# First chunk of `w_in` loaded first, min(r, 1)^2 of eight chunks as a square on ScalarE, other work shares

## The chip, the cores and the metric

The kernel runs on one core of one Trainium2 chip. The metric is the device time of one execution in microseconds (us). Engines are named as in the profile: PE is TensorE's matmul, PEld its weight load, DVE is VectorE, ACT is ScalarE, POOL is GpSimd, SP is SyncE, which here only issues DMAs.

## The reference

Sigmoid attention for 8 batches of 12 heads (448 tokens, head width 64), followed by a two-layer MLP over all 3584 tokens. The activation between the two layers is 0 below -1, h above 1, and (h+1)^2/4 between.

```python
scores = scale * np.matmul(q, k.transpose(0, 1, 3, 2)) - np.log(S)
attn = 1.0 / (1.0 + np.exp(-scores))
x = np.ascontiguousarray((attn @ v).transpose(0, 2, 1, 3)).reshape(B * S, H * D)
h = x @ w_in                       # 768 -> 2048
g = np.where(h >= 1, h, np.where(h <= -1, 0.0, (h + 1) ** 2 / 4.0))
return g @ w_out                   # 2048 -> 768
```

## The kernel before

**Tiling.** One batch is one tile of 448 tokens. Two heads make a pair (48 pairs, six for a batch). For each pair, `scores` fills `psc` from K and Q in three pieces of 128 keys and one of 64, ACT takes the sigmoid in `weigh` (L454 or L457), and `av` adds the product with V into `pav`; ACT copies it to `x32` (L504) and DVE takes its largest value (L508). The hidden width is 16 chunks of 128. For a batch, `up` (L722, or `up_blocks` L688 from batch 2 on, a scheme with seven instead of eight products) makes h of each chunk in PSUM (`ph`, three banks shared with `po`), `bend` turns h into g and splits g into two f16 halves `ghl`, and `down` (L758) adds the chunks into `po`, which DVE scales into `o` (L768).

**Two f16 halves.** Nearly every matmul runs on high and low f16 halves, three products each. So each operand needs a largest value, a scale, a rounded copy (mostly ACT) and a remainder (mostly DVE, `SCALAR_TENSOR_TENSOR`).

**The weights.** They come as 64-bit words. `Weight.load` (L202) fetches a chunk of 768 KB, and `Weight.convert` makes f32 of it: ACT takes the absolute value (L224), a clamp follows (L226, on POOL for chunks 0, 2, 4 and 6, later on DVE; or together with the maximum in L236), and three DVE operations of 768 columns put the bits together (L241, L244, L247). Eight chunks of `w_in` have their bound summed by ACT (L218). `find_scale` and `split` then make the f16 halves (L286, L287, or L282 to L284 on POOL).

**The order in time.** Batch 0's attention (f32 matmuls, pairs 0 to 5) runs beside the conversion of `w_in`; when its six pairs are done, `finish_x(0)` scales x. Then batch 0's 16 chunks of `up` and its first-half `down` run, interleaved with batch 1's attention and the conversion of `w_out`: 72 units in all, and `B0`, `B1` say over which of them the attention steps are spread. Batch 1's MLP is interleaved with batch 2's attention up to `LAST1` units before its end, and with `mix`, which prepares the blocks of `w_in` that `up_blocks` reads. From batch 2 on each batch does 56 block units and 48 `down` units beside the next batch's attention. `L0`, `A0`, `LSTEP` say at which attention step pairs 8 and 9 are loaded and prepared ahead of time.

**Shares.** `prep_a` finds the largest or summed absolute values of a pair from 8 on: for pairs below `MAX_ACT` by ACT with a sum (L344, two or three instructions), for the others by DVE with `tensor_reduce` (L346, two instructions). `prep_b` splits q, k and v of a pair: by ACT and DVE below `QA` (L373, L374), by POOL above (L378 to L380).

**What sets the order.** SP's first loads are written out by hand; within an engine, a list scheduler places the rest by priority and its own estimate of time, so the order of instructions changes everywhere when a part changes. Each engine runs its list in order: an instruction that waits holds back all behind it.

`bend` before, for a chunk whose h stands in PSUM: ACT makes r in `g` by a Relu with a bias (L735); DVE makes min(r, rt)·r (L736), where rt is the value that stands for 1; DVE takes the larger of that and h times a factor (L737), which is the last reader of the PSUM bank; ACT rounds (L738); DVE takes the remainder (L739).

Of the kernel before, what the change touches and what calls it, by code (L numbers as in the profile page):

```python
# [14 lines left out]
F32 = mybir.dt.float32  # L15
# [3 lines left out]
AF = mybir.ActivationFunctionType  # L19
ALU = mybir.AluOpType  # L20
# [18 lines left out]
LAST = 84  # L39
LAST1 = 18  # L40
WI_A = 14
# [3 lines left out]
B0 = 9  # L45
B1 = 66
GPOOL = 1
POOL_FROM = 6
WI_SUM = 2
WO_SUM = 0  # L50
MAX_ACT = 47
L0 = 9
A0 = 19
LSTEP = 3

SB = 2
CLAMP = 7
QA = 17
QT = 3
WOP = 6  # L60
MIXP = 0
CORN = 10
TP = 1

DW = 8
# [10 lines left out]
def sigmoid_attention_mlp(ctx: ExitStack, tc: tile.TileContext, first_qvk, qkv, w_in, w_out, out_t):  # L76
# [102 lines left out]
    class Weight:  # L179


        def __init__(self, dram, sb, name, spare):
            self.dram, self.sb, self.name, self.spare = dram.bitcast(I32), sb, name, spare
            self.words, self.at, self.loaded = {}, 0, 0
            self.scale, self.inv = [], []
            self.most = const.tile([P, 2, NFC], F32, name=name + "_most")
            nc.vector.memset(self.most, 0.0)
            mod = WI_SUM if name == "wi" else WO_SUM
            self.summed = [f for f in range(NFC) if mod and f % mod == 0 and f not in (NA - 1, NFC - 1)]

# [19 lines left out]
        def convert(self):  # L210

            f = self.at - 2
            if 0 <= f < NFC:
                w = self.words.pop(f)
                if f in self.summed:

                    dump = wo.f32(-1) if self is wi else w[:, :DM].bitcast(F32)
                    nc.scalar.activation(dump, self.f32(f), AF.Abs, accum_out=self.most[:, 1, f : f + 1])  # L218
                if self is wo:
                    self.load(3 if f == 3 else 1)  # L220
# [33 lines left out]
        def find_scale(self):  # L254
# [4 lines left out]
            nc.vector.tensor_reduce(out=m, in_=self.most[:, :, GROUPS[k]], axis=AX.X, op=ALU.max)  # L259
            c, e = m[:, 0:1], sml_p.tile([P, 1], F32, tag="wx", name=name + "_x", bufs=1)  # L260
            ci, ei = c.bitcast(I32), e.bitcast(I32)
# [291 lines left out]
    def small(tag, in0, s1, op0, s2=None, op1=None, ints=False):  # L553
        t = sml_p.tile([P, 1], F32, tag=tag, name=tag, bufs=2 if tag.startswith("od") else 1)
# [43 lines left out]
    def common_scales(b, inv_x, ih=None):  # L598

        big = [largest(inv_x, k) for k in range(2)]  # L600
        q = [small("q%d" % k, big[k][1], wo.root[k], ALU.mult) for k in range(2)]
        q = small("qm", q[0], q[1], ALU.min)
        for k in range(2):
            up_sc[b, k] = up_scales(ih or big[k][0], small("rk%d" % k, q, wo.iroot[k], ALU.mult), k)
        od = inverse("od", small("qq", q, q, ALU.mult))
        down_sc[b, None] = lambda: od
# [19 lines left out]
    def mix(i):  # L626
# [25 lines left out]
        for t0, n, chunk, k in ((0, 2, f, 0), (2, 1, g, 1)):  # L652
            src = w_in_sb[:, chunk].rearrange("p h (t n) -> p h t n", t=2)[:, :, 2 - n :, :]
            for h in range(2):
                nc.vector.tensor_scalar(
                    out=pv[:, h, t0 : t0 + n, :], in0=src[:, h], scalar1=to[k], scalar2=None, op0=ALU.mult
                )
        nc.sync.dma_start(out=blocks[i][:, : 3 * DM], in_=pl)
# [70 lines left out]
    def bend(b, f, h):  # L729
# [4 lines left out]

        nc.scalar.activation(g, h, AF.Relu, bias=hr, scale=ihr)  # L735
        nc.vector.scalar_tensor_tensor(out=g, in0=g, scalar=rt, in1=g, op0=ALU.min, op1=ALU.mult)  # L736
        nc.vector.scalar_tensor_tensor(out=g, in0=h, scalar=ihs, in1=g, op0=ALU.mult, op1=ALU.max)  # L737
# [5 lines left out]
    def down(b, m, u, k):  # L743

        lo, hi = (0, NFC) if k is None else (GROUPS[k].start, GROUPS[k].stop)
        if u == 0:
            hold["po"] = ps_mo.tile([P, 512], F32, tag="mo", name="po")
            hold["o"] = out_p.tile([P, S], F32, tag="o", name="o")
            if m == 0:
                hold["od"] = down_sc[b, k]()  # L750
            if k == 1:
                nc.sync.dma_start(out=hold["o"], in_=part[m])
        po, o = hold["po"], hold["o"]

# [72 lines left out]

    with tc.manual_schedule(engines={mybir.EngineType.SP}):
        load_pair(0)
        wi.load(1, nc.sync)  # L830
        load_pair(1)
        wi.load(2, nc.sync)
        load_pair(2)
        wi.load(3, nc.sync)
        for i in range(LAG):
# [131 lines left out]
```

## Time and profile before

| what | value |
|---|---|
| three runs | 1188.74, 1192.86, 1194.42 us; median 1192.86 |
| the profiled execution | 1187.38 us, of it 1185.7 us span and 1.7 us around it |
| PE busy | 1144.9 us (97% of the span) |
| DVE busy | 854.9 us (72%) |
| ACT busy | 697.6 us (59%) |
| POOL busy | 332.8 us (28%) |
| DMA | 170.01 MB, mean 143 GB/s |

How to read it: the PE row says that the matmul engine is nearly always at work, so time can only be won where it is not. The page cuts the span into 40 slices; a digit below 9 in the PE row marks such a place. The profiled execution was 5.5 us faster than the median of the three runs.

### The profile page before, as it was taken

To read this page: it belongs to the slowest core of one execution; us is meant where nothing else is said; L and a number is where in the kernel's file an instruction comes from. 1 tells how busy PE (TensorE), PEld (TensorE's weight loads), DVE (VectorE), ACT (ScalarE), POOL (GpSimd) and SP (SyncE) were. 2 spreads that over 40 slices of the span, in tenths; PEclk is the share of its full clock that TensorE was granted. 3 is DMA by queue.
4 is the path that set the end of the run, shared out by engine and by line. 5 is a ranking of instruction groups with operands and counts; after the bars stand their busy time and mean duration, and the time that the engine had idled before them with its cause. 6 is when DMAs were issued, how large, how long until landed. Compare 5 with 4: busy or idle time off the path is not lost.

```text
span 1185.7 us, 20268 instructions
## 1 busy us (share of the span) xinstructions
PE 1144.9 (97%) x7662; PEld 669.3 (56%) x7662; DVE 854.9 (72%) x1828; ACT 697.6 (59%) x1158; POOL 332.8 (28%) x393
## 2 busy tenths in 40 slices
PE   5889899999999999999999999999999999999998
PEld 1224333444445776457754677557764577558954
DVE  6999999999956588457973689456884678736830
ACT  5886576665654577547864578455864476613510
POOL 3004410011323244234345235332532353310000
PEclk9899999999999999999999999999999999999999
DMA  9842354437542266224643065423552246302400
GB/s 367 322 153 76 118 161 152 134 119 257 182 148 72 95 217 210 76 72 142 238 163 102 30 236 208 135 64 128 204 211 64 65 147 220 126 24 87 163 16 32
DMA packets 58113, 170.01 MB, mean 143 GB/s; under 512 B 8608, under 2 KB 39840, under 8 KB 51872
## 3 DMA queue, kind: packets, MB, share of 16 engines
q1 hardware_dynamic: 56288, 159.29, 39.1%
q10 hardware_dynamic: 1728, 9.44, 2.2%
q8 instruction: 60, 0.98, 0.3%
q14 instruction: 37, 0.30, 0.1%
HBM read 126.94 MB, written 23.40 MB: 127 GB/s over the span
## 4 chain that ended last, share of the span: by engine, by line
PE 71%; DVE 17%; DMA 4%; ACT 3%; issue 2%; POOL 2%; SPq 0%; POOLq 0%; ACTq 0%; DVEq 0%
PE po L758 33%; PE ph L688 22%; PE pav L498 8%; PE psc L416 3%; PE psc L425 2%; PE ph L722 2%; DVE g L736 2%; PE psc L411 1%; DVE g L737 1%; DVE ghl L739 1%; DMA raw<-qkv 1%; DVE ahl L466 1%; DVE w_in_sb L244 1%; DVE mixa L632 1%; DVE w_out_sb L247 1%
## 5 line engine op out<-in xcount | busy, mean ns | idle before, releaser
L758 PE MATMUL po<-ghl,w_out_sb 128*128 128x448 f16 x2304 | 446.3, 353 | 1.5 <-DVE qkv_e L131 0.6
L758 PEld LDWEIGHTS <-w_out_sb 128*128 128x128 f16 x2304 | 221.7, 98 | 219.4 <-issue 15.9
L688 PE MATMUL ph<-w_in_sb 128*128 128x224 f16 x3024 | 307.7, 259 | 1.3 <-DVE g L737 0.9
L688 PEld LDWEIGHTS <-w_in_sb 128*128 128x128 f16 x3024 | 282.6, 98 | 30.1 <-issue 27.2
L466 DVE SCALAR_TENSOR_TENSOR ahl<-psc,ahl 128x896 f16<-128x896 f32 (+1 forms) x170 | 153.0, 900 | 105.7 <-ACT ahl L465 103.6
L378 POOL TENSOR_SCALAR raw<-raw,qkv_s 128x448 f32<-128x448 f32 (+1 forms) x93 | 71.0, 777 | 449.9 <-DVE qkv_i L139 346.3
L457 ACT ACTIVATE psc<-psc,nls,sqk 128x896 f32<-128x896 f32 (+1 forms) x136 | 129.5, 971 | 103.5 <-PE psc L425 86.6
L465 ACT ACTIVATE ahl<-psc 128x896 f16<-128x896 f32 (+1 forms) x170 | 126.9, 762 | 29.8 <-DVE ahl L466 28.6
L722 PE MATMUL ph<-xhl,w_in_sb 128*128 128x448 f16 x576 | 114.5, 356 | 4.7 <-DVE g L737 3.4
L344 ACT ACTIVATE dump<-raw 128x448 f16<-128x448 f32 (+1 forms) x105 | 61.9, 589 | 85.8 <-DMA raw<-qkv 84.5
L697 DVE TENSOR_TENSOR xhl<-ph,xhl 128x224 f32<-128x224 f32 x240 | 87.7, 383 | 25.3 <-PE ph L688 19.4
L738 ACT ACTIVATE ghl<-g 128x448 f16<-128x448 f32 x128 | 72.5, 573 | 44.2 <-DVE g L737 43.8
L498 PE MATMUL pav<-ahl,v 128*64 128x448 f16 x748 | 95.6, 360 | 0.0
L735 ACT ACTIVATE g<-xhl,hr,ihr 128x448 f32<-128x448 f32 x96 | 68.7, 752 | 41.9 <-DVE xhl L697 41.0
L722 PEld LDWEIGHTS <-w_in_sb 128*128 128x128 f16 x576 | 55.7, 99 | 63.6 <-issue 14.4
L736 DVE SCALAR_TENSOR_TENSOR g<-g,rk 128x448 f32<-128x448 f32 x112 | 81.4, 741 | 10.2 <-ACT g L735 10.0
L739 DVE TENSOR_TENSOR ghl<-g,ghl 128x448 f16<-128x448 f32 x128 | 85.0, 672 | 5.3 <-ACT ghl L738 4.8
L768 DVE TENSOR_SCALAR o<-po,od 128x448 f32<-128x448 f32 x48 | 32.5, 679 | 61.1 <-PE po L758 60.8
L380 POOL TENSOR_TENSOR hl<-raw,hl 128x448 f16<-128x448 f32 x62 | 71.1, 1167 | 0.0
L416 PE MATMUL psc<-qk 128*128 128x448 f16 x252 | 66.3, 354 | 2.0 <-ACT a L454 1.0
L737 DVE SCALAR_TENSOR_TENSOR g<-xhl,ihs,g 128x448 f32<-128x448 f32 x96 | 66.3, 708 | 0.3
L498 PEld LDWEIGHTS <-v 128*64 128x64 f16 x748 | 36.3, 109 | 37.9 <-issue 23.0
(167 smaller groups left out, 1198.5 us busy)
## 6 DMA issues: line engine op xcount, KB each, us to landing
w_in_sb<-blocks SPq DMA_DIRECT2D x48, 1344.0 KB, 6.1
raw<-qkv SPq DMA_DIRECT2D x34, 704.0 KB, 4.7
qk<-hl SPq DMA_DIRECT2D x320, 56.0 KB, 2.0
w_out_sb<-w_in SPq DMA_DIRECT2D x16, 768.0 KB, 8.5
out_t<-o SPq DMA_DIRECT2D x48, 224.0 KB, 1.9
blocks<-mixs SPq DMA_DIRECT2D x8, 768.0 KB, 3.5
w_out_sb<-w_out ACTq DMA_DIRECT2D x6, 768.0 KB, 4.1
raww<-w_out ACTq DMA_DIRECT2D x6, 768.0 KB, 5.7
```

Source lines behind the costliest of these rows:

```text
L416: nc.tensor.matmul(out, kq[:, j, 1, w], kq[:, j, 0, :], start=True, stop=False)
L457: nc.scalar.activation(a, a, AF.Sigmoid, bias=nls, scale=sqk)
L465: nc.scalar.activation(hi, x, AF.Copy, scale=ATT)
L466: nc.vector.scalar_tensor_tensor(out=lo, in0=x, scalar=ATT, in1=hi, op0=ALU.mult, op1=ALU.subtract)
L498: nc.tensor.matmul(pav[j * D : (j + 1) * D, :S], *terms[j][t], start=c == 0 and t == 0, stop=mid and t == len(terms[j]) - 1,)
L688: nc.tensor.matmul(out, w[:, wt, wh, c * P : (c + 1) * P], xc[:, xt, c, xh, :], start=j in (0, 2) and c + wh + xh == 0, stop=c == HC - 1 a ...
L697: add = lambda out, q, other: nc.vector.tensor_tensor(out=out, in0=quarter(q), in1=other, op=ALU.add)
L722: nc.tensor.matmul(ph[:, :S], w_in_sb[:, f, wh, c * P : (c + 1) * P], xhl[:, c, xh, :], start=c == 0 and wh + xh == 0, stop=c == NCC - 1 a ...
L736: nc.vector.scalar_tensor_tensor(out=g, in0=g, scalar=rt, in1=g, op0=ALU.min, op1=ALU.mult)
L737: nc.vector.scalar_tensor_tensor(out=g, in0=h, scalar=ihs, in1=g, op0=ALU.mult, op1=ALU.max)
L739: (nc.gpsimd if f % GPOOL else nc.vector).tensor_tensor(out=ghl[:, f, 1, :], in0=g, in1=hi, op=ALU.subtract)
L758: nc.tensor.matmul(po[:, :S], w_out_sb[:, f, wh, m * P : (m + 1) * P], ghl[:, f, gh, :], start=f == lo and wh + gh == 0, stop=f == hi - 1 ...
```

## The change

It has these parts.

- **Load order.** Before, SP issued pair 0, one chunk of `w_in`, pair 1, two chunks, pair 2, three chunks. Now it issues one chunk, a pair and one chunk, three times over.
- **Early sigmoid.** A sigmoid of one column (`spare`) stands first on ACT, so that the one table load that is left happens before any data is there.
- **Square.** For chunks 0, 2, ..., 14 of batch 0 (eight of 16), the DVE instruction of L736 goes. ACT's first Relu gets the negated scale `mi` (made by a one-column DVE operation for each half of the chunks) and gives rt - min(r, rt); a second ACT Relu with scale -1 and bias rt gives min(r, rt); a third ACT instruction squares it. For h below 1 that is the old product; above, L737 takes its other argument as before.
- **Shares.** `MAX_ACT` 47 to 17 (pairs 17 to 46 get their largest values from DVE instead of ACT), `QA` 17 to 18 (pair 17 is split by ACT and DVE instead of POOL), `B1` 66 to 68, `LAST1` 18 to 17, `L0` 9 to 11, `LSTEP` 3 to 2.
- Several new switches (`AM`, `MIXA`, `CUT`) leave the program as it was at the values given, and some one-column buffers share a name.

```diff
-LAST1 = 18
+LAST1 = 17
-B1 = 66
+B1 = 68
-MAX_ACT = 47
-L0 = 9
+MAX_ACT = 17
+L0 = 11
-LSTEP = 3
+LSTEP = 2
-QA = 17
+QA = 18
+    if EARLY:
+        spare = const.tile([P, 1], F32, name="spare")
+        nc.scalar.activation(spare, nls, AF.Sigmoid)
...
+    def minus_scale(b, k):
+        if b < SQ:
+            minus_sc[b, k] = small("mi%d" % k, up_sc[b, k][0], -1.0, ALU.mult)
...
-        nc.scalar.activation(g, h, AF.Relu, bias=hr, scale=ihr)
-        nc.vector.scalar_tensor_tensor(out=g, in0=g, scalar=rt, in1=g, op0=ALU.min, op1=ALU.mult)
+        if b < SQ and f % SQM == 0:
+            nc.scalar.activation(g, h, AF.Relu, bias=hr, scale=minus_sc[b, int(f >= NA)])
+            nc.scalar.activation(g, g, AF.Relu, bias=rt, scale=-1.0)
+            nc.scalar.activation(g, g, AF.Square)
+        else:
+            nc.scalar.activation(g, h, AF.Relu, bias=hr, scale=ihr)
+            nc.vector.scalar_tensor_tensor(out=g, in0=g, scalar=rt, in1=g, op0=ALU.min, op1=ALU.mult)
...
+            for k in range(3):
+                wi.load(1, nc.sync)
+                load_pair(k)
+                wi.load(1, nc.sync)
```

The first place is the start of SP's list. `L202` (now `L214`) is a chunk of `w_in`; `L316` and `L317` (now `L328` and `L329`) are the two DMAs of a pair. Before:

```order
L316 DMA ghl<-first_qvk 128x2x448
L317 DMA ghl<-first_qvk 128x448
L202 DMA w_out_sb<-w_in 128x1536
L316 DMA ghl<-first_qvk 128x2x448
L317 DMA ghl<-first_qvk 128x448
L202 DMA w_out_sb<-w_in 128x1536 x2
```

Now:

```order
L214 DMA w_out_sb<-w_in 128x1536
L328 DMA ghl<-first_qvk 128x2x448
L329 DMA ghl<-first_qvk 128x448
L214 DMA w_out_sb<-w_in 128x1536 x2
L328 DMA ghl<-first_qvk 128x2x448
L329 DMA ghl<-first_qvk 128x448
```

The first chunk moved ahead of pair 0, the third ahead of pair 1.

The second place is ACT's list at the same time and, behind it, at the first bends of batch 0. Its start before:

```order
L224 ACT_TABLE_LOAD
L224 ACTIVATE w_in_sb<-w_out_sb 128x768
L454 ACT_TABLE_LOAD
L454 ACTIVATE a_123<-psc,nls 128x896
L454 ACTIVATE a_128<-psc,nls 128x896
L224 ACTIVATE w_in_sb<-w_out_sb 128x768
```

Its start now (`L236` is the old `L224`, `L466` the old `L454`):

```order
L114 ACT_TABLE_LOAD
L114 ACTIVATE spare<-nls 128x1
L236 ACTIVATE w_in_sb<-w_out_sb 128x768 x2
L466 ACTIVATE a_125<-psc,nls 128x896
L227 ACTIVATE w_out_sb,wi_most<-w_in_sb 128x768
```

One table load is gone, and the first sigmoid now stands behind the absolute values of two chunks. At batch 0's first bends ACT has now (`L758` to `L760` are the new three, `L762` the old `L735`, `L765` the old `L738`):

```order
L758 ACTIVATE g<-ph,hr_549,mi_551 128x448
L762 ACTIVATE g<-ph,hr_549,ihr_547 128x448
L759 ACTIVATE g<-g,ru_541 128x448
L760 ACTIVATE g<-g 128x448
L466 ACTIVATE a_895<-psc,nls,sqk 128x896
L214 DMA w_out_sb<-w_out 128x1536
L765 ACTIVATE ghl<-g 128x448 x2
```

Two more ACT instructions stand between the first Relu of such a chunk and its rounding, with other ACT work between them.

The third place is DVE's list where a batch's last block of `up_blocks` is bent (batch 3). `L697` adds quarters of h, `L156` prepares the sum of a pair's largest values over the partitions. Before:

```order
L697 TENSOR_TENSOR xhl<-ph,xhl 128x224 x2
L736 SCALAR_TENSOR_TENSOR g<-g,rk_5145 128x448
L736 SCALAR_TENSOR_TENSOR g<-g,rk_5135 128x448
L737 SCALAR_TENSOR_TENSOR g<-xhl,ihs_5149,g 128x448
L737 SCALAR_TENSOR_TENSOR g<-xhl,ihs_5139,g 128x448
L156 CAST mb<-m_6479 128x3
L739 TENSOR_TENSOR ghl<-g,ghl 128x448 x2
```

Now (`L763`, `L764`, `L766` are the old `L736`, `L737`, `L739`; `L358` is the old `L346`, `L167` the old `L156`):

```order
L763 SCALAR_TENSOR_TENSOR g<-g,rk_5136 128x448
L478 SCALAR_TENSOR_TENSOR ahl<-psc,ahl 128x896
L766 TENSOR_TENSOR ghl<-g,ghl 128x448
L764 SCALAR_TENSOR_TENSOR g<-xhl,ihs_5140,g 128x448
L763 SCALAR_TENSOR_TENSOR g<-g,rk_5126 128x448
L358 TENSOR_REDUCE m_6462<-raw 128x2
L358 TENSOR_REDUCE m_6462<-raw 128x1
L764 SCALAR_TENSOR_TENSOR g<-xhl,ihs_5130,g 128x448
L766 TENSOR_TENSOR ghl<-g,ghl 128x448
```

The two reductions of a later pair, which read a freshly loaded tile `raw`, now stand ahead of the last chunk's L764 and L766.

More of the change, by code (lines that the diff above doesn't have):

```diff
@@ L63 @@
 TP = 1
+EARLY = 2
+SQ = 1
+SQM = 2
+SLAG = 2
+AM = 0
+MIXA = 0
+CUT = 8
 DW = 8
@@ L187, in __init__ @@
             nc.vector.memset(self.most, 0.0)
-            mod = WI_SUM if name == "wi" else WO_SUM
-            self.summed = [f for f in range(NFC) if mod and f % mod == 0 and f not in (NA - 1, NFC - 1)]
+            mod = WI_SUM if name == "wi" else 0
+            early = [f for g in GROUPS for f in range(g.start, g.stop - SLAG + 1)]
+            self.summed = [f for f in early if mod and f % mod == 0]
         def f32(self, f):
@@ L210, in convert @@
         def convert(self):
+            f = self.at - SLAG
+            if 0 <= f < NFC and f in self.summed:
+                nc.scalar.activation(wo.f32(-1), self.f32(f), AF.Abs, accum_out=self.most[:, 1, f : f + 1])
             f = self.at - 2
             if 0 <= f < NFC:
[L214 to L218, printed above, removed]
+                self.words.pop(f)
                 if self is wo:
@@ L259, in find_scale @@
             nc.vector.tensor_reduce(out=m, in_=self.most[:, :, GROUPS[k]], axis=AX.X, op=ALU.max)
-            c, e = m[:, 0:1], sml_p.tile([P, 1], F32, tag="wx", name=name + "_x", bufs=1)
+            c, e = m[:, 0:1], sml_p.tile([P, 1], F32, tag="xm1", name=name + "_x", bufs=1)
             ci, ei = c.bitcast(I32), e.bitcast(I32)
@@ L553, in small @@
     def small(tag, in0, s1, op0, s2=None, op1=None, ints=False):
-        t = sml_p.tile([P, 1], F32, tag=tag, name=tag, bufs=2 if tag.startswith("od") else 1)
+        t = sml_p.tile([P, 1], F32, tag=tag, name=tag, bufs=2 if tag == "od" else 1)
         o, i = (t.bitcast(I32), in0.bitcast(I32)) if ints else (t, in0)
@@ L604, in common_scales @@
             up_sc[b, k] = up_scales(ih or big[k][0], small("rk%d" % k, q, wo.iroot[k], ALU.mult), k)
-        od = inverse("od", small("qq", q, q, ALU.mult))
+            minus_scale(b, k)
+        od = inverse("od", small("gb", q, q, ALU.mult))
         down_sc[b, None] = lambda: od
@@ L654, in mix @@
             for h in range(2):
-                nc.vector.tensor_scalar(
-                    out=pv[:, h, t0 : t0 + n, :], in0=src[:, h], scalar1=to[k], scalar2=None, op0=ALU.mult
-                )
+                if MIXA:
+                    nc.scalar.activation(pv[:, h, t0 : t0 + n, :], src[:, h], AF.Copy, scale=to[k])
+                else:
+                    nc.vector.tensor_scalar(
+                        out=pv[:, h, t0 : t0 + n, :], in0=src[:, h], scalar1=to[k], scalar2=None, op0=ALU.mult
+                    )
         nc.sync.dma_start(out=blocks[i][:, : 3 * DM], in_=pl)
@@ L746, in down @@
         if u == 0:
-            hold["po"] = ps_mo.tile([P, 512], F32, tag="mo", name="po")
-            hold["o"] = out_p.tile([P, S], F32, tag="o", name="o")
+            hold["po", m] = ps_mo.tile([P, 512], F32, tag="mo", name="po")
+            hold["o", m] = out_p.tile([P, S], F32, tag="o", name="o")
             if m == 0:
@@ L751, in down @@
             if k == 1:
-                nc.sync.dma_start(out=hold["o"], in_=part[m])
-        po, o = hold["po"], hold["o"]
+                nc.sync.dma_start(out=hold["o", m], in_=part[m])
+        po, o = hold["po", m], hold["o", m]
         pair = (u, u + NFC // 2) if b >= SB else (lo + 2 * u, lo + 2 * u + 1)
@@ L788, in downs @@
         n = NFC if k is None else GROUPS[k].stop - GROUPS[k].start
-        return [lambda m=m, u=u: down(b, m, u, k) for m in range(NCC) for u in range(n // 2)]
+        order = [(m, u) for m in range(NCC) for u in range(n // 2)]
+        if b >= SB:
+            first = [(m, u) for m in range(2) for u in range(CUT)] + [(m, u) for m in range(2) for u in range(CUT, n // 2)]
+            order[: n] = first
+        return [lambda m=m, u=u: down(b, m, u, k) for m, u in order]
     def step(i):
@@ L826, in convert @@
                 wo.load(2, nc.sync)
[L828 to L834, printed above, removed]
+    with tc.manual_schedule(engines={mybir.EngineType.SP} | ({mybir.EngineType.Activation} if AM else set())):
+        if EARLY > 1:
+            for k in range(3):
+                wi.load(1, nc.sync)
+                load_pair(k)
+                wi.load(1, nc.sync)
+        else:
+            load_pair(0)
+            wi.load(1, nc.sync)
+            load_pair(1)
+            wi.load(2, nc.sync)
+            load_pair(2)
+            wi.load(3, nc.sync)
         for i in range(LAG):
```

7 lines of the change are left out of this document (4 added, 3 removed).

## The prediction

> **What bounds the kernel now.** I read the page's slices first, then busy time by stage, then the waits stage by stage. The first rows are the page's: each digit is the busy share of a fortieth of the span.
>
> ```profile
> PE   5889899999999999999999999999999999999998
> DVE  6999999999956588457973689456884678736830
> ```
>
> PE is below 9 only in the first slices, DVE is at 9 just there. The second view gives busy time in five stretches that I cut at DVE's start, at the end of batch 0's attention, where PE becomes full, and at two batch borders (columns: stretch, its length, then busy us and instructions of PE, PEld, DVE, ACT and POOL, granted clock, DMA share, GB/s).
>
> ```profile
> 0.00:11.20 11.20, 3.35 (x8) 1.18 (x8) 0.20 (x4) 4.38 (x5) 2.83 (x7) 1.00 0.83 296
> 11.20:90.00 78.80, 62.58 (x236) 16.27 (x236) 76.98 (x139) 62.56 (x93) 6.83 (x3) 0.89 0.75 280
> 90.00:255.00 165.00, 154.56 (x773) 66.54 (x772) 156.16 (x331) 108.19 (x170) 34.64 (x25) 0.99 0.36 122
> 255.00:394.00 139.00, 138.64 (x780) 68.33 (x780) 103.05 (x213) 77.01 (x126) 33.99 (x41) 1.00 0.48 156
> 394.00:1078.00 684.00, 682.72 (x5082) 440.76 (x5079) 471.63 (x1048) 420.30 (x721) 254.52 (x318) 1.00 0.40 138
> ```
>
> From 255 to 1078 us PE is idle for 0.36 + 1.28 us: nothing can be won there, and a gain made earlier is kept. Before 255 PE is idle for 7.9, 16.2 and 10.4 us, and DVE is the full engine: 76.98 of 78.80 us and 156.16 of 165. So a microsecond that DVE gets back before 255 us is worth up to one at the end. In its first 11.2 us DVE does nothing, for this reason (wait rows: who waited for whom, us in total, times, longest):
>
> ```profile
> DVE w_in_sb L241 <- POOL w_in_sb L226: 10.7, 2, 10.1
> PE ph L722 <- DVE g L737: 3.4, 3, 1.8
> PE pm L159 <- DVE g L737: 3.2, 2, 2.6
> ```
>
> The other two are PE's longest waits from 90 to 255 us: both are for batch 0's bends.
>
> **The change part by part. Load order.** The timeline of the start (start us, us, engine, line, operation) and the DMA rate in 40 slices of the first 12 us:
>
> ```profile
> 1.80 0.42 SPq L202 DMA_DIRECT2D w_out_sb<-w_in  x1
> 4.46 3.35 PE L407 MATMUL psc<-ghl 64*128 64x448 f32 x8 [4.46 <-DMA ghl<-first_qvk]
> 8.07 0.89 ACT L224 ACTIVATE w_in_sb<-w_out_sb 128x768 f32<-128x768 f32 x1 [5.99 <-DMA w_out_sb<-w_in]
> 8.98 1.28 ACT L454 ACT_TABLE_LOAD   x1
> 9.05 2.13 POOL L226 TENSOR_SCALAR w_in_sb<-w_in_sb 128x768 f32<-128x768 f32 x1 [7.67 <-ACT w_in_sb L224]
> 10.27 1.91 ACT L454 ACTIVATE a<-psc,nls 128x896 f32<-128x896 f32 x2
> 11.21 0.56 DVE L241 TENSOR_SCALAR w_in_sb<-w_in_sb 128x768 int32<-128x768 int32 x1 [10.13 <-POOL w_in_sb L226]
> 12.07 0.90 ACT L224 ACTIVATE w_in_sb<-w_out_sb 128x768 f32<-128x768 f32 x1
> GB/s 0 0 0 0 0 0 90 173 299 311 382 365 388 452 300 313 266 369 348 384 286 328 271 292 346 358 387 377 410 432 466 416 410 471 389 389 471 430 410 370
> ```
>
> Pair 0 (672 KB, 0.688 MB) has landed at 4.46 us and the first chunk (768 KB, 0.786 MB) at 8.07. Adding up the slices (0.3 us each), 0.83 MB had moved by the first time and 2.0 MB by the second, so of what had moved 83% and, with pair 0, 73% belonged to what was waited for. With the same shares the chunk alone needs 0.95 to 1.08 MB, reached at 4.9 to 5.3 us: I take 5.1, that is 3.0 us earlier. Abs and POOL's clamp follow as now, and DVE begins at 8.2. The bits of one chunk keep it for 2.5 us (0.56 and twice 0.96), to 10.7. The second chunk is now third in the queue: 2.26 MB by the same shares is 2.7 to 3.1 MB moved, at 10 to 10.8 us, and its Abs takes 0.9. So DVE has a hole of about 0.5 us, and **2.5 us** are left of the 3.0. The ends: 0 if the transfers share the engines so that the chunk lands no sooner, 3.6 if it lands when pair 0 did.
>
> The first sigmoid now stands behind both Abs, so at some 11.2 instead of 10.27 us. One table load of 1.28 us has left ACT's way. I put this at nothing: in the stretch to 90 us PE has 16 us and ACT 16 us to spare, and they cover the 0.9 us; without that cover it costs 0.9.
>
> **Squares.** The groups of 90 to 255 us (line, operation, shape, count, then busy us, mean ns, idle before):
>
> ```profile
> L735 ACT ACTIVATE g<-ph,hr,ihr 128x448 f32<-128x448 f32 x22 | 15.5, 714 | 7.6 <-PE ph L722 7.5
> L736 DVE SCALAR_TENSOR_TENSOR g<-g,ru 128x448 f32<-128x448 f32 x16 | 12.9, 811 | 0.7 <-ACT g L735 0.7
> L738 ACT ACTIVATE ghl<-g 128x448 f16<-128x448 f32 x21 | 11.7, 572 | 12.7 <-DVE g L737 12.7
> ```
>
> Eight of the 16 L736 go: 8 x 0.811 = 6.5 us less on DVE. The trace shows neither the second Relu nor the square; they lie between 0.572 (no pointer operands) and 0.714 (two of them), so ACT gets 8 x 1.14 to 1.43 = 9 to 11 us more, and is then busy for 118 of 165 us instead of 108. Behind them in ACT's list stand sigmoids and roundings for which PE waits little. A chunk's own chain grows by 0.33 to 0.62 us plus what stands between in ACT's list. At most the whole 6.5 reaches PE; at worst PE waits for the longer chain of eight chunks, 8 x 0.62 = 5.0 us lost. I take a gain of **4.0**, nearer to the upper end because the rows name DVE as what PE and even ACT (12.7 us before L738) wait for.
>
> The Trainium skill speaks against this part: "ScalarE: Activation LUTs", section "Rules for kernel authors", has relu, max and mul on VectorE and not on ScalarE. The rows agree for one instruction (0.811 against two of at least 0.572). By that rule the sum would lose 2.6 to 5.0 us where I gain 4; it is the third rival below.
>
> **Largest values on DVE.** A pair's rows (durations min/median/max in ns), the DVE form from pair 47:
>
> ```profile
> L346 DVE TENSOR_REDUCE m<-raw x2: 676/881/1086, 985.5 to 986.5; 128x2 f32<-128x896 f32 x1, 128x1 f32<-128x512 f32 x1
> L344 ACT ACTIVATE dump<-raw x105: 559/577/640, 152.8 to 977.5; 128x448 f16<-128x448 f32 x72, 128x512 f16<-128x512 f32 x33
> L344 ACT ACTIVATION_READ_ACCUMULATOR dump<-raw x105: 185/187/217, 153.2 to 978.0; 128x1 f32 x105
> 394.00:470.00 76.00, 76.00 (x674) 58.16 (x670) 63.80 (x135) 57.87 (x104) 35.64 (x44) 1.00 0.52 181
> 470.00:531.00 61.00, 61.00 (x347) 30.06 (x347) 30.57 (x79) 28.52 (x49) 18.19 (x24) 1.00 0.28 94
> ACT dump L344 <- DMA raw<-qkv: 14.6, 3, 7.0
> DVE mb L156 <- ACT dump L344: 9.9, 2, 7.3
> ```
>
> DVE gets 1.76 us for each of 30 pairs, ACT loses 3 x 0.76 = 2.3. In a batch like the one from 394 to 531 us the block stage is the tight one: DVE 63.8 of 76 us, and three pairs make it 69. It still fits, and the `down` stage is half empty. The wait for the load moves from ACT to DVE, with the rest of a bend queued behind it; but DVE waited already, for ACT's dump of the same load (9.9 us in a batch, the last two rows, of 531 to 668 us). So nothing is gained or lost while PE stays full; the ends are a gain of 0.5 (PE's one wait for a rounding) and the loss of the second rival.
>
> **The other shares** go together at 0, within 2 us either way: pair 17 costs DVE some 2 us at a time (255 to 394) when it has 36 to spare, and frees POOL; B1 stretches batch 1's attention by two units, LAST1 leaves 17 instead of 18 units of 6 matmuls to cover the last scaling, and L0 and LSTEP move two loads by a few steps. PE's work is the same throughout.
>
> **Sum.** 2.5 + 4.0 = 6.5 us off the profiled execution's 1187.38 (span 1185.7 and 1.7 around it): 1180.9. That execution lies 5.5 us under the median of the runs shown, 1192.86, and I give the forecast on the median: **1186.4 us**.
>
> **The rivals.**
>
> 1. *Only one of the two terms arrives.* Against it: DVE is full on both sides of 90 us, so the early start should carry over. For it, two more stretches, in which ACT is as full as DVE, so that x of batch 0 may wait for ACT instead:
>
> ```profile
> 45.00:60.00 15.00, 13.14 (x55) 3.31 (x51) 14.57 (x37) 14.27 (x24) 0.00 (x0) 0.95 0.71 240
> 60.00:75.00 15.00, 12.99 (x58) 3.73 (x60) 15.00 (x25) 14.84 (x22) 0.00 (x0) 1.00 0.68 224
> 90.73 3.45 ACT L521 ACTIVATE xhl<-x,x_s 128x448 f16<-128x448 f32 x6
> ```
>
>    Gain 2.5 to 4: 1190.
> 2. *The bend of a batch's last chunk waits for a load.* The reductions now stand ahead of that chunk's L737 and L739, and PE has to read the chunk's g within the first `down` units. For it:
>
> ```profile
> 610.14 0.58 ACT L344 ACTIVATE dump<-raw 128x448 f16<-128x448 f32 x1 [1.50 <-DMA raw<-qkv]
> 613.14 0.17 DVE L156 CAST mb<-m 128x3 bf16<-128x3 f32 x1 [2.59 <-ACT dump L344]
> 613.61 0.62 DVE L739 TENSOR_TENSOR ghl<-g,ghl 128x448 f16<-128x448 f32 x1 [0.29 <-ACT ghl L738]
> PE po L758 <- ACT ghl L738: 0.5, 1, 0.5
> ```
>
>    The load lands only at 610.1, and PE has already waited 0.5 us at such a place. Against it: DVE stood still until 613.14 there, and with the reductions it would go on at 610.1 + 1.76 = 611.9. It decides if the load lands over 1.2 us later than now against DVE's list. At 1.76 + 1.50 = 3.3 us in each of the five batches from 2 on that have such pairs it costs 16 beside the forecast's gain: 1203, slower.
> 3. *The longer ACT chain eats the squares.* PE waits for L737 of the squared chunks, 2.6 to 5.0 us: 1192.86 - 2.5 + 3.8 = 1194.
> 4. *The full effect.* Both terms at their upper ends, 3.6 + 6.5, and up to 2 of the other shares: 1181 to 1183.
> 5. *The chunk lands no sooner*, because all transfers of the first microseconds share the DMA engines: the change does not do what it says, and the squares alone give 1189.
>
> **How the numbers follow.** Forecast 0.45, rival 1 0.17, rival 2 0.10, rival 3 0.08, rival 4 0.14, rival 5 0.06. A measurement of this kernel can tell some 0.5%, here 6 us, from no change. The forecast's own spread (4.5 to 9) lies for three quarters beyond 6: with rival 4 that makes faster 0.48; rivals 1, 3 and 5 and the rest of the forecast make 0.42; rival 2 makes slower 0.10. The range reaches from rival 4 less the scatter of the runs (4 us under the median) to rival 3 and the scatter above it: 1177 to 1196.
>
> **What would show it.** Right: DVE's first L241 near 8.2 us; x of batch 0 scaled (L521, the row above) some 2.5 us before 90.7; PE's waits for L737 from 90 to 255 us fall well under 6.6; the first block matmul (L688) comes 5 to 8 us before 394; 137 us a batch from there on, as now. Wrong: a DVE hole of over 1 us after the first chunk; PE waits at the first `down` units of each batch; new PE waits on ACT's square.

## The result and the profile after

The change makes the kernel **slower**: median 1211.44 us (1208.48 to 1212.38, four runs) against 1190.80 us (1188.32 to 1194.42, four runs), a ratio of 1.0173 with a 95% interval of 1.015 to 1.0196. The four of before are the three shown above and one more. The profiled executions differ by 24.9 us (span 1185.7 and 1210.6), 4 us more than the medians, since the profiled one of before lies 3.4 us under its median. One execution of one experiment, the profiled one of the reductions undone, took 3915.93 us; it stands in no median, and no trace of that run is read.

The page's slices of the changed kernel (PE and DVE busy in tenths, and the clock granted to PE):

```profile
PE   5689999899899999999999999999999999999998
DVE  6997997898895599666994789747995579736830
PEclk8799999899999999999999999999999999999999
```

DVE's row of nines in the first 300 us is broken, and PE's row, which had nothing but nines from 150 us to the last slice, has an 8 at 212 to 242 us and one at 303 to 333 us. The five stretches of before, for the changed kernel:

```profile
0.00:11.20 11.20, 3.88 (x10) 1.70 (x12) 3.06 (x8) 4.57 (x6) 2.83 (x7) 1.00 0.83 317
11.20:90.00 78.80, 57.81 (x211) 14.34 (x207) 72.70 (x127) 58.70 (x88) 7.34 (x3) 0.85 0.73 270
90.00:255.00 165.00, 155.41 (x749) 64.42 (x746) 141.14 (x308) 111.69 (x172) 32.39 (x24) 0.97 0.35 116
255.00:394.00 139.00, 132.95 (x735) 64.38 (x734) 117.83 (x228) 73.44 (x109) 28.83 (x32) 1.00 0.50 164
394.00:1078.00 684.00, 673.07 (x5040) 435.71 (x5039) 511.33 (x1081) 375.76 (x568) 246.83 (x316) 1.00 0.40 138
```

From 11.2 to 90 us PE, DVE and ACT have done less than before: PE 57.8 us of work instead of 62.6, DVE 72.7 instead of 77.0, ACT 58.7 instead of 62.6. From 255 us on PE, which had no holes, has some.

Where the 24.9 us arise is seen from the start of the same instruction in both traces (us; `x` scaled is the first L521, now L533; the 145th `down` matmul is the first of batch 0's second half; the block matmul is L688, now L709):

| instruction | before | after | difference |
|---|---|---|---|
| first Abs of `w_in` | 8.07 | 5.12 | -2.9 |
| x of batch 0 scaled | 90.7 | 95.3 | +4.6 |
| x of batch 1 scaled | 222.8 | 227.8 | +5.0 |
| 145th matmul of `down` | 260.9 | 270.4 | +9.5 |
| 289th matmul of `down` | 329.7 | 346.3 | +16.6 |
| first block matmul | 394.4 | 411.4 | +17.0 |
| the same, five batches on | 1077.9 | 1102.6 | +24.7 |

So 4.6 us are lost ahead of 95 us, 12 between 228 and 346, and 7.7 in five batches that take 691.2 instead of 683.5 us.

PE's longest wait from 11.2 to 90 us, before and then after (who waited for whom, us in total, times, longest):

```profile
PE psc L407 <- ACT a L454: 14.4, 7, 3.5
```

```profile
PE psc L419 <- ACT a L466: 19.0, 10, 3.5
```

In batch 0's attention PE waits more for sigmoids, though the first comes at 9.6 us, sooner than the 10.3 of before. PE's longest wait from 90 to 255 us, and what DVE does there (timeline):

```profile
PE ph L743 <- DVE xhl L534: 4.2, 1, 4.2
```

```profile
226.90 0.15 DVE L568 TENSOR_SCALAR rt<-gb 128x1 int32<-128x1 int32 x1
229.80 0.96 DVE L650 TENSOR_TENSOR mixa<-w_in_sb 128x768 f32<-128x768 f16 x1 [2.75 <-DMA blocks<-mixs]
...
231.67 1.01 DVE L299 SCALAR_TENSOR_TENSOR w_out_sb<-w_out_sb,wo_s 128x768 f16<-128x768 f32 x1
232.59 0.20 DVE L568 TENSOR_SCALAR q<-ru,root 128x1 f32<-128x1 f32 x1
232.72 0.67 DVE L534 SCALAR_TENSOR_TENSOR xhl<-x,x_s,xhl 128x448 f16<-128x448 f32 x1
```

PE needs the low half of batch 1's x (L534). It stands in DVE's list behind L650, the preparation of a block of `w_in`, which waits 2.75 us for a DMA. Before, the old L650 stood behind the low halves, and PE waited 0.4 us there. From 411 to 1103 us PE's first wait and DVE's of the load are:

```profile
PE ph L709 <- DVE xhl L718: 6.2, 10, 0.7
```

```profile
DVE m L358 <- DMA raw<-qkv: 30.5, 15, 5.1
```

L718 adds the quarters of h; twice a batch it comes 0.6 us late. It shares DVE's list with the reductions L358.

### The profile page after: what moved, and what is told of

It reads as the page before. It is cut to its first block, busy times and chain, and to the rows that moved or that the text cites. A ratio compares the mean times of both kernels' runs of the same rounds, so it can differ in the third digit from the quotient of the medians.

```text
span 1210.6 us, 20115 instructions
## 1 busy us (share of the span) xinstructions
PE 1150.9 (95%) x7662; PEld 669.4 (55%) x7662; DVE 907.7 (75%) x1885; ACT 655.3 (54%) x997; POOL 321.4 (27%) x384
## 4 chain that ended last, share of the span: by engine, by line
PE 60%; DVE 21%; DMA 8%; POOL 4%; issue 4%; ACT 2%; SPq 1%; ACTq 0%; POOLq 0%; DVEq 0%
PE po L785 30%; PE ph L709 14%; PE pav L510 6%; DMA raw<-qkv 4%; PE ph L743 3%; DVE g L764 3%; PE psc L428 3%; DVE g L763 2%; PE psc L437 2%; DVE ahl L478 2%; DVE ghl L766 2%; DMA w_in_sb<-blocks 1%; DVE xhl L718 1%; DVE m L358 1%; PE psc L423 1%
## 5 line engine op out<-in xcount | busy, mean ns | idle before, releaser
L709 PE MATMUL ph<-w_in_sb 128*128 128x224 f16 x3024 | 306.8, 259 | 9.1 <-DVE xhl L718 6.2
L709 PEld LDWEIGHTS <-w_in_sb 128*128 128x128 f16 x3024 | 284.1, 98 | 37.7 <-issue 31.4
L390 POOL TENSOR_SCALAR raw<-raw,qkv_s 128x448 f32<-128x448 f32 (+1 forms) x90 | 64.4, 731 | 435.3 <-issue 297.3
L743 PE MATMUL ph<-xhl,w_in_sb 128*128 128x448 f16 x576 | 115.8, 359 | 11.2 <-DVE xhl L534 4.2
L765 ACT ACTIVATE ghl<-g 128x448 f16<-128x448 f32 x128 | 73.0, 575 | 92.5 <-DVE g L764 92.0
L718 DVE TENSOR_TENSOR xhl<-ph,xhl 128x224 f32<-128x224 f32 x240 | 87.0, 381 | 19.3 <-PE ph L709 15.5
L762 ACT ACTIVATE g<-xhl,hr,ihr 128x448 f32<-128x448 f32 x96 | 68.7, 754 | 48.3 <-DVE xhl L718 41.8
L763 DVE SCALAR_TENSOR_TENSOR g<-g,rk 128x448 f32<-128x448 f32 x112 | 86.0, 778 | 6.0 <-ACT g L762 6.0
L766 DVE TENSOR_TENSOR ghl<-g,ghl 128x448 f16<-128x448 f32 x128 | 85.0, 673 | 4.7 <-ACT ghl L765 4.2
L358 DVE TENSOR_REDUCE m<-raw 128x2 f32<-128x896 f32 (+1 forms) x62 | 51.9, 878 | 42.7 <-DMA raw<-qkv 42.6
L764 DVE SCALAR_TENSOR_TENSOR g<-xhl,ihs,g 128x448 f32<-128x448 f32 x96 | 74.8, 793 | 0.1
L392 POOL TENSOR_TENSOR hl<-raw,hl 128x448 f16<-128x448 f32 x60 | 65.2, 1109 | 0.0
L419 PE MATMUL psc<-ghl 64*128 64x448 f32 (+1 forms) x128 | 39.2, 704 | 25.4 <-ACT a L466 19.0
```

What stands on the lines that cost most here:

```text
L709: nc.tensor.matmul(out, w[:, wt, wh, c * P : (c + 1) * P], xc[:, xt, c, xh, :], start=j in (0, 2) and c + wh + xh == 0, stop=c == HC - 1 a ...
L718: add = lambda out, q, other: nc.vector.tensor_tensor(out=out, in0=quarter(q), in1=other, op=ALU.add)
L743: nc.tensor.matmul(ph[:, :S], w_in_sb[:, f, wh, c * P : (c + 1) * P], xhl[:, c, xh, :], start=c == 0 and wh + xh == 0, stop=c == NCC - 1 a ...
L766: (nc.gpsimd if f % GPOOL else nc.vector).tensor_tensor(out=ghl[:, f, 1, :], in0=g, in1=hi, op=ALU.subtract)
```

## Experiments

All times are medians; where two runs are compared, 2 to 3 us is what their scatter allows to tell. The start of the profiled executions scatters too: with the old loads the first Abs comes at 8.0 to 9.5 us.

### One part undone in the changed kernel

```diff
-MAX_ACT = 17                    # run 1
+MAX_ACT = 47
-EARLY = 2                       # run 2
+EARLY = 0
-SQ = 1                          # run 3
+SQ = 0
-QA, B1, LAST1, L0, LSTEP = 18, 68, 17, 11, 2   # run 4, five lines
+QA, B1, LAST1, L0, LSTEP = 17, 66, 18, 9, 3
```

> The changed kernel with MAX_ACT back at 47: the largest values of pairs 17 to 46 come from ACT again, all else as changed. Theory A (DVE's reduction stands in its list and waits for the pair's load, so that bends behind it come late): the batches from 394 us on take 137.2 us again instead of 138.8, and of the 17 us lost ahead of 394 us the 7 lost between 255 and 394 come back too; about 1197 us. Rival B (the loss sits in the start and in the list scheduler's other order, not in the reductions): the batches stay at 138.8 and the time at 1209 to 1213.

> The changed kernel with EARLY at 0: SP's first loads in the old order and no early sigmoid, all else as changed. Theory A (the new order brings chunks of w_in at the cost of pairs 1 and 2, so batch 0's attention falls behind): x of batch 0 is scaled at some 91 us again instead of 95.3, and 4 to 5 us of the 20 come back: about 1207 us. Rival B (what holds batch 0 back is another part, such as the loads put off by L0): x stays at 95 us and the time at 1211. Rival C (the early start was a gain that another part hides): slower than 1211 by up to 2.5 us.

> The changed kernel with SQ at 0: no squares on ACT, L763 on DVE for all 16 chunks of batch 0, all else as changed. Theory A (the squares do what was forecast, DVE being full from 90 to 255 us, and are not part of the loss): some 4 us slower, 1215 us. Rival B (the longer chain on ACT costs PE time, 2.6 to 5 us): 1206 to 1209 us. Rival C (neither, DVE has time to spare there): 1211 us.

> The changed kernel with the small shares back (QA 17, B1 66, LAST1 18, L0 9, LSTEP 3), all else as changed. Theory A (they are worth nothing, within 2 us): 1209 to 1213 us. Rival B (the later loads of pairs 8 and 9 by L0 and pair 17's split on DVE make the bubbles at 225 to 255 and 290 to 340 us): the first block matmul comes 8 to 12 us before 411 us, and the time is 1199 to 1203 us.

Measured: 1203.22, 1208.67, 1216.56 and 1211.97 us against 1211.44. Undoing the reductions gives back **8.2** us, the loads **2.8** (at the edge of what the scatter allows to tell), the squares cost **5.1** when taken away, and the shares make no difference. Theory A holds for the squares and shares. For the other two it holds in direction: the reductions give back 8 us where 14 were expected, and the loads less than the 4 to 5: x of batch 0 is back at 90.7 us with the old loads, but x of batch 1 comes only 1.1 us sooner.

### One part alone

The base is a kernel with all parts undone by their switches. It is not quite the kernel before: some one-column buffers stay shared, to make room for the negated scales.

```diff
-            ... sml_p.tile([P, 1], F32, tag="wx", name=name + "_x", bufs=1)
+            ... sml_p.tile([P, 1], F32, tag="xm1", name=name + "_x", bufs=1)
-        t = sml_p.tile([P, 1], F32, tag=tag, name=tag, bufs=2 if tag.startswith("od") else 1)
+        t = sml_p.tile([P, 1], F32, tag=tag, name=tag, bufs=2 if tag == "od" else 1)
-        ... small("od%d" % k, inverse("ig%d" % k, sc[4]), wo.inv[k], ALU.mult)
+        ... small("od1" if k else "od", inverse("ig", sc[4]), wo.inv[k], ALU.mult)
-        od = inverse("od", small("qq", q, q, ALU.mult))
+        od = inverse("od", small("gb", q, q, ALU.mult))
```

> All parts undone by their switches (EARLY 0, SQ 0, MAX_ACT 47, the small shares as before): what is left of the change is that some one-column tiles share a buffer. Theory A (the shared buffers cost nothing): the time before, 1191 us within 3. Rival B (they add waits on DVE, or change the order, and carry some of the loss): over 1194 us.

> The kernel before (with the shared one-column buffers) with MAX_ACT at 17 alone. Theory A (the reductions wait in DVE's list for the load, with bends behind them): batches from 394 us on at 138.8 instead of 137.2 us and a loss of 8 to 15 us, 1199 to 1206 us. Rival B (the loss is not theirs): 1191 us.

> The kernel before (with the shared one-column buffers) with the new load order and the early sigmoid alone. Theory A (pairs 1 and 2 come later and batch 0's attention, which ACT and the pieces of x set, falls behind): x of batch 0 scaled 4 to 5 us after 90.7, and the time 1194 to 1196 us. Rival B (the early start is a gain, as forecast): x 2.5 us before 90.7, and 1188 to 1189 us.

> The kernel before (with the shared one-column buffers) with the small shares alone (QA 18, B1 68, LAST1 17, L0 11, LSTEP 2). Theory A (nothing, within 2 us): 1189 to 1193 us. Rival B (they make the bubbles at 225 to 255 and 290 to 340 us): 8 to 12 us lost ahead of the first block matmul, 1199 to 1203 us.

Measured: the base 1194.74 us, ratio to before 1.0035 (1.0011 to 1.0059): what is left, above all the **shared buffers**, costs about 4 us (rival B; by the interval 1 to 7). The trace of the base has as many instructions on each engine as the one before, in another order on DVE from 76 us on. Over the base, the reductions cost **7.1** us (1201.80), the loads **12.0** (1206.71; x at 96.8 us, a little later than theory A had it, and the time 11 us above it) and the shares **4.3** (1199.08: rival B's time, but since the base itself lost 4, with only 3 us lost ahead of the first block matmul). Together that is more than the 20.6 us lost: the parts don't add up, since each changes the whole order. The loads cost 12.0 alone and 2.8 beside the others.

The squares alone, in the kernel before, with no other buffer shared (two tiles lose a second buffer that is never used):

> The kernel before with the eight squares alone; the room for the two negated scales comes from two one-column tiles that had a second buffer without use, no other tile is shared. Theory A (the square takes 6.5 us from DVE, which is full from 90 to 255 us; undoing it in the changed kernel cost 5.1 us): faster, 1186 us, ratio 0.996, and x of batch 1 is scaled 4 us before 222.8. Rival B (the gain is only there beside the other parts, since in the kernel before DVE's list has other holes there): 1190 to 1192 us. Rival C (the longer ACT chain costs): over 1193 us.

1194.86 us, 3.2 us over the 1191.69 of before in the same series, ratio 1.003 (1.0014 to 1.0047): a small loss in place of the gain. The time is rival C's, its longer chain is not seen: PE's waits for the bends (L737 by its old number) from 92 to 232 us are 3.4 us, after 4.2 in the kernel before. In the base the squares do no better:

> All parts undone but the squares, with the shared one-column buffers. Theory A (squares are worth 4 to 5 us, as they were beside all other parts; what the run of the squares alone lost came from another order at 255 to 340 us): x of batch 1 scaled 3 to 4 us sooner after x of batch 0 than without (133.5 us), time 1190 us. Rival B (squares gain only where other parts have made DVE late): x of batch 1 133 us or more after x of batch 0, and 1193 to 1196 us.

1194.35 us, and x of batch 1 comes 133.5 us after x of batch 0, as in the base: rival B by the numbers. The trace of this run shows where the gain goes. DVE and, behind the fence, PE:

```profile
219.68 1.83 DVE L650 TENSOR_TENSOR mixa<-w_in_sb 128x768 f32<-128x768 f16 x2 [2.58 <-DMA blocks<-mixs]
221.42 0.68 DVE L795 TENSOR_SCALAR o<-po,od 128x448 f32<-128x448 f32 x1
222.02 0.28 DVE L187 TENSOR_REDUCE xm<-pm 128x1 f32<-128x128 f32 x1
...
224.92 0.15 DVE L146 TENSOR_SCALAR x_s<-x_e 128x1 int32<-128x1 int32 x1
```

```profile
226.25 1.28 PE L743 MATMUL ph<-xhl,w_in_sb 128*128 128x448 f16 x3 [4.51 <-ACT xhl L533]
```

The same L650 stands here ahead of batch 1's largest value (L187), so the scale `x_s`, and with it x, is late, and PE waits 4.5 us, about what was to be gained. Up to there the squares had gained: the last step ahead of that largest value (L529) comes 118.4 us after x of batch 0 is scaled, in the base 125.6. L529 here and, behind the fence, in the base:

```profile
210.41 0.15 DVE L529 TENSOR_REDUCE xm<-xm 128x1 f32<-128x6 f32 x1
```

```profile
214.82 0.15 DVE L529 TENSOR_REDUCE xm<-xm 128x1 f32<-128x6 f32 x1
```

From L529 to L187 it takes 11.6 us here and 3.1 in the base. L650 with its wait is 4.4 of the 11.6, the rest is other work, most of it on the weights. That this order is the cause is read from the trace; no run took it away.

### Why the loads hold batch 0 back

Four readings were open: the early sigmoid, the first chunk ahead of pair 0, the later places of pairs 1 and 2, and ACT's list that follows from any of these.

```diff
-EARLY = 0       # base; first run
+EARLY = 1
-            load_pair(0)        # second run
-            wi.load(1, nc.sync)
+            wi.load(1, nc.sync)
+            load_pair(0)
-WI_SUM = 2      # third run, on the new loads alone
+WI_SUM = 0
```

> The kernel with all parts undone (shared one-column buffers) with the early sigmoid alone, the loads in the old order. Theory A (what holds batch 0's attention back is where pairs 1 and 2 stand in the load queue): 1193 to 1196 us like the kernel with all parts undone, x of batch 0 scaled at 88 to 91 us. Rival B (the table load that comes early changes the list scheduler's order so that ACT's sums stand ahead of sigmoids): x at 95 to 97 us, 1202 to 1207 us.

> The kernel with all parts undone (shared one-column buffers) with only the first chunk ahead of pair 0; pairs 1 and 2 keep their place (chunk, pair 0, pair 1, two chunks, pair 2, three chunks), no early sigmoid. Theory A (pairs 1 and 2 behind one and two more chunks were the harm, the first chunk a gain): x of batch 0 scaled at 87 us and 1191 to 1193 us. Rival B (pair 0 behind a chunk is the harm itself, since ACT's sigmoids start the chain of batch 0 and are what x waits for): x at 92 to 97 us, over 1198 us. Rival C (the start makes no difference, DVE being full anyway): 1194 to 1196 us.

> The new load order and early sigmoid as in their run alone (1206.7 us, x of batch 0 scaled at 96.8 us), but no chunk of w_in has its bound summed by ACT: DVE finds the largest value together with the clamp instead (some 1 us more for eight chunks), ACT's eight sums of 1.0 us and their waits for DVE go. Theory A (sigmoids of batch 0 stand behind ACT's sums, and those wait for DVE's conversion): PE's waits for sigmoids (25 us ahead of 100 us) fall to under 16 and x comes at 90 us or sooner. Rival B (the pairs' places in the load queue, or a DMA-bound start, hold batch 0 back): x at 95 us or later, as DVE has 8 us more to do.

The early sigmoid is harmless (1194.05 us, theory A). The first chunk ahead of pair 0 is enough for the whole harm (1205.08 us, x at 98.3, rival B), so the places of pairs 1 and 2 are not needed for it. Without ACT's sums 5 us come back (1201.63), but x stays late at 96.0, as rival B has it: for x the sums were not it. What the late ones share is seen in ACT's list. The kernel before, and then the changed one, around the first rounding of `w_in` (L286, now L298):

```profile
47.91 1.01 ACT L454 ACTIVATE a<-psc,nls 128x896 f32<-128x896 f32 x1 [0.70 <-PE psc L407]
...
49.64 0.92 ACT L286 ACTIVATE w_in_sb<-w_in_sb,wi_s 128x768 f16<-128x768 f32 x1
```

```profile
46.77 0.99 ACT L466 ACTIVATE a<-psc,nls 128x896 f32<-128x896 f32 x1
47.66 0.53 ACT L516 ACTIVATE x<-pav 128x448 f32<-128x448 f32 x1
49.49 0.94 ACT L298 ACTIVATE w_in_sb<-w_in_sb,wi_s 128x768 f16<-128x768 f32 x1 [1.29 <-DVE wi_s L146]
```

The rounding starts at 49.5 to 49.6 us in both, but before it ACT has done 13 sigmoids then and 10 now, and now it even waits for the scale. In all runs but the two that follow and the one whose trace is not read:

| loads | sigmoids ahead of the first rounding | it starts at | x of batch 0 |
|---|---|---|---|
| a pair first (before and ten runs) | 13 | 49.5 to 51.5 | 89.2 to 92.5 |
| a chunk first (after and five runs) | 10 | 48.2 to 50.2 | 95.3 to 98.3 |

So with a chunk first the list scheduler puts the first rounding ahead of three sigmoids, as if the conversion were done sooner. It isn't. From 11 to 50 us the DMA engines are full in the base and with the new loads alone (stretch, length, busy of PE, PEld, DVE, ACT, POOL, clock, DMA share, GB/s):

```profile
11.00:50.00 39.00, 28.97 (x98) 7.38 (x98) 37.90 (x69) 28.26 (x47) 6.92 (x4) 0.82 1.01 397
```

```profile
11.00:50.00 39.00, 23.24 (x80) 5.75 (x82) 35.83 (x61) 24.34 (x41) 7.33 (x3) 0.84 1.00 385
```

The ninth chunk's last conversion step (L259) starts at 39.6 and 39.8 us: the 2.9 us of the start are used up by 40 us.

To tell list from loads, ACT's list was kept in the order of the program for both load orders (the rounding then has 17 sigmoids ahead of it in both traces; the 18 below counts a table load with them):

```diff
-AM = 0          # both runs; the second also has EARLY = 2
+AM = 1
```

> All parts undone, and ACT's list in batch 0's attention kept in the order of the program (the switch AM), in which 18 sigmoids instead of 13 stand ahead of the first rounding of w_in (L298). It is the base for the next run. Theory A (where the first rounding stands among the sigmoids decides when batch 0's attention ends): x of batch 0 is scaled at 92 us or sooner, though the first chunk's Abs stands behind seven sigmoids and the conversion begins late. Rival B (the conversion's start decides): x later than 95 us.

> The new load order and the early sigmoid, with ACT's list in batch 0's attention kept in the order of the program as in the run beside it (17 sigmoids ahead of the first rounding). With the scheduler's list (10 ahead) the same loads brought x of batch 0 at 96.8 us. Theory A (the list, not the loads, held batch 0 back): x within 2 us of the run beside it, and the time within 3 us of it. Rival B (pairs 0 to 2 behind chunks in the load queue hold it back): x 5 to 8 us later than in the run beside it, and 5 to 12 us slower.

1211.60 and 1208.89 us, x at 103.9 and 104.3. With the list the same, the loads move x by 0.4 us and cost nothing (theory A of the second run). Theory A of the first run fell: 17 sigmoids ahead are no better than 10, as DVE gets its first chunk only at 16.9 us there. So the count marks a list; it is no rule. And that list is itself so slow that it could hide a delay by the loads. PE's waits to 100 us with the new loads alone, under the scheduler's own list, speak against such a delay:

```profile
PE psc L419 <- ACT a L466: 25.2, 12, 3.9
PE psc L419 <- DMA ghl<-first_qvk: 6.5, 1, 6.5
```

PE waits for a pair's load once, for the first one, 2.2 us longer than in the base (4.3); what doubles are its waits for sigmoids, from 13.0 us to 25.2. **It is the list rather than the loads** that holds batch 0 back, by this reading. Not shown is which place in the list does it: no run has the new loads with the base's own list.

### What the reductions cost

```diff
             if late:                                  # first run, on the reductions alone
-                prep_a(p + 3)
+                if p + 3 < MAX_ACT: prep_a(p + 3)
+            if 17 <= p < MAX_ACT:                     # second run, on the base
+                src = ready[p - 2][4] as f32          # shortened
+                nc.vector.tensor_reduce(out=idle, in_=src of 2 x 448, ...)
+                nc.vector.tensor_reduce(out=idle[:, 0:1], in_=src[:, :512], ...)
```

> The kernel with all parts undone but MAX_ACT at 17 (as in the run of the reductions alone, 1201.8 us), and in addition the reductions of a pair from 17 on stand half a pair later in the program, when its load has long landed. Theory A (the 7 us are the wait for the load, with the quarters of h and the bends queued behind it): DVE's waits for the load (28.2 us from 400 to 1090 us) go to under 5, PE's waits for DVE's quarters (6.2 us, 10 times) go, and the time to 1195 us. Rival B (the 1.7 us of DVE work of each pair itself holds the quarters back, landed or not): PE's waits stay at 5 to 7 us and the time at 1200 to 1203 us.

> All parts undone (ACT finds the largest values), plus two DVE reductions of 896 and 512 columns for each of the 30 pairs from 17 on, over a tile that has been ready for a pair's time; their results go nowhere. The reductions alone, which read the fresh load, took 1201.8 us against 1194.7. Theory A (the DVE work itself, 1.7 us a pair in the stage of the blocks, makes the quarters of h late): PE waits for DVE's quarters some 5 to 7 us in all from 400 us on, as with the reductions, and 1199 to 1203 us. Rival B (the wait for the load is what costs): no such waits, 1194 to 1196 us.

The first took 1203.34 us and tells nothing: the scheduler put the reductions where they had been, as DVE's waits of the run with the reductions alone and of this one show (400 to 1090 us):

```profile
DVE m L358 <- DMA raw<-qkv: 28.2, 14, 5.4
```

```profile
DVE m L358 <- DMA raw<-qkv: 28.2, 14, 5.3
```

The second took 1201.14 us, as much as the reductions (1201.80): by the time, theory A. Its trace speaks for rival B: PE's only wait from 394 to 1090 us is this, not for quarters, and five batches take 685.3 us as in the base, where the reductions make them 688.8. The first block matmul comes 2.7 us later than in the base, with the reductions as with the extra work.

```profile
PE psc L433 <- DVE qkv_e L142: 0.9, 2, 0.5
```

But the profiled execution was the fastest of its four (1198.1, the others 1200.5 to 1202.3). And the extra reductions did not find their tile ready, as the run had meant: DVE waits for POOL's split in front of them, longer than the real ones wait for the load (400 to 1090 us):

```profile
DVE idle L362 <- POOL hl L397: 50.5, 20, 5.5
```

So this run does not keep the work apart from a wait, and it isn't settled by which of the two the reductions cost. It does show that DVE can wait for 50 us in these batches without PE waiting for quarters. Shown is that 30 pairs of reductions cost 7 to 8 us. With the reductions alone DVE's busy time in a stage of blocks is near the 69 of 76 us of the forecast, but PE, which was full there, is idle for 1.5 us:

```profile
403.00:479.00 76.00, 74.55 (x669) 57.66 (x668) 67.77 (x137) 53.42 (x85) 32.65 (x42) 1.00 0.51 179
```

### The stretch from 255 to 345 us

```diff
-MIX1 = 85
+MIX1 = 95
```

> All parts undone (1194.7 us, 73.9 us between the 145th and 289th matmul of L785 where the kernel before takes 68.8), with the preparation of the blocks of w_in spread to unit 95 instead of 85 of batch 1. Theory A (DVE is full from 255 to 340 us, so what it does first there is what PE waits for, and a mere change of the order costs 4 to 7 us; fewer blocks in that stretch give it back): that distance at 69 to 71 us, first block matmul at 394 to 397 us, 1189 to 1192 us. Rival B (the blocks come late for batch 2): PE waits for blocks before the first block matmuls, over 1196 us.

The distance falls to 69.7 us as theory A says, but the first block matmul comes at 401.9 (400.2 in the base) and the time is 1197.95 us, not faster than the base; the 3 us above it are at the edge of the scatter. What that stretch gains is lost ahead of it: x of batch 0 comes 3.2 us later than in the base, x of batch 1 another 1.6 (135.1 us after x of batch 0 instead of 133.5). PE's waits for blocks, rival B, don't show. No kernel of this study is faster than the one before.

## Why the prediction was wrong

The forecast was 1186.4 us (1177 to 1196), measured are 1211.44. Two steps failed. One is that a gain before 255 us is kept to the end because DVE is the full engine: the early start came as said, and x of batch 0 was 4.6 us later, not 2.5 sooner. The other is that the reductions cost nothing because they still fit into DVE's stretch: they cost 7 to 8 us. The parts don't add up, so the 20.6 us lost can't be shared out among them in full.

- **Load order, -2.5 forecast; +2.8 beside the other parts, +12.0 alone.** Its first signs were right: Abs at 5.1, DVE's first L241 at 8.3 where 8.2 was said, and not even the hole of 0.5 us behind the first chunk. The step that failed leads from "DVE is the full engine" to "a microsecond that DVE gets back before 255 us is worth up to one at the end". A busy share of 77 of 79 us doesn't say that DVE sets the end: up to 50 us the DMA engines were just as full, ACT's list serves both the attention and the conversion, and with the changed list DVE itself fell to 72.7. The rows of 45 to 75 us in the first rival, with ACT at 14.3 to 14.8 of 15 us, were the sign of it, but priced as a lost gain, not as a loss.
- **The first sigmoid, at nothing because 16 us are spare.** It came even sooner than forecast (9.6, not 11.2). Alone, with the old loads, it changed nothing, as forecast (1194.05 against 1194.74). But beside the new loads PE's waits for sigmoids rose from 14.4 to 19.0 us, though the spare time was real as a sum: holes don't cover what comes in the wrong order.
- **Squares, -4.0 forecast; -5.1 beside the other parts, nothing (-0.4) in the base, +3.2 alone in the kernel before.** The costs on ACT were right: the second Relu takes 0.662 and the square 0.574 us, 8 x 1.24 = 9.9 us where 9 to 11 were said. So was the sign at the bends: PE's waits for L737 (now L764) from 90 to 255 us fell from 6.6 to 2.0 us, and no PE wait on the square shows. By the rule of the Trainium skill ("ScalarE: Activation LUTs", section "Rules for kernel authors") relu, max and mul belong on VectorE. For the single instruction the rows agree (0.811 us there, 1.24 here); what the exchange is worth in time hangs on the order, by the three figures above. What failed is again "kept": without the other parts, L650 and the work beside it take the gain back at x of batch 1, by the trace.
- **Largest values on DVE, 0 forecast; +7 to 8.** The step that failed is "three pairs make it 69. It still fits". DVE's busy time came as said (67.8 us with the reductions alone), and still PE loses 1.5 us in that stage: room in the sum is no sign that each quarter comes in time. The place was named in the second rival (3.3 us at the end of each batch's bends, 16 in all); what came is 0.7 us a batch with the reductions alone (against the base) and 1.5 in the changed kernel (against the kernel before), mostly at quarters in the middle of the blocks, and the rest ahead of the first block matmul. PE's waits at the first `down` units, its sign, are only 1.3 us in five batches.
- **Other shares, 0 within 2; +4.3 alone, -0.5 beside the others.** The bounds were too narrow for the first; that the second lies within them is luck, since the same lines cost 4.3 in another order.
- **Not in the sum at all: the shared buffers, +4 us.** They add no instruction and change the order.
- The range and the rivals had one slow case, by a wait at one place. A new order of all engines' lists was no rival, and the runs point to it: from 255 to 394 us, where "nothing can be won", PE is idle for 0.4 us in the kernel before, for about 1 in two other runs (the early sigmoid, and `MIX1` at 95), and for 2.1 to 6.4 us in all the rest whose trace is read.

## What to carry to other kernels

A busy share near 100% names an engine to look at, not the bound: a gain is kept only if the next thing waited for at the following border (here x of a batch) also comes sooner, so read what stands ahead of that in each list. Where a scheduler lays out in-order lists, price a change of a number as a change of the whole order, with both signs, and look in the new lists for instructions that wait for a DMA ahead of the ones PE needs. Try each part of a bundle alone and taken out: here the sum of the single effects was not the effect of all.

## What the runs showed of the hardware

From 50 to 90 us (base, the new loads alone, ACT's list fixed) the granted clock is lower where PE is less busy:

```profile
50.00:90.00 40.00, 35.08 (x151) 9.42 (x148) 39.56 (x77) 35.88 (x50) 0.00 (x0) 0.96 0.53 171
```

```profile
50.00:90.00 40.00, 30.30 (x109) 7.57 (x105) 37.56 (x66) 31.81 (x43) 0.00 (x0) 0.82 0.49 160
```

```profile
50.00:90.00 40.00, 20.02 (x70) 5.57 (x70) 35.94 (x61) 27.78 (x42) 0.00 (x0) 0.76 0.44 157
```

That goes with the Trainium skill ("TensorE: Matmul & The Clock Gate", section "Part 1: The HAM clock gate"), by which the clock follows how busy PE has been recently. But busy time over such a stretch does not give the clock: from 11 to 50 us the rows further up have 0.82 at 28.97 us busy in the base and 0.84 at 23.24 with the new loads alone.

In the first 60 us the median f32 matmul of `psc` takes 640 ns in the base and 714 with the new loads alone. How much of the time lost in PE's waits is lost once more by slower matmuls is not shown.
